# Second roundings behind the masks, banks by age, thresholds of the first steps on ScalarE, and a piece of MLP work between turning and values

## The chip, the cores and the metric

The kernel runs on one core of a Trainium2 chip. The metric is the device time in microseconds of one execution. The profile comes from one execution of its own; its span runs from the first to the last instruction.

## What is computed

Attention with a threshold, followed by a two-layer MLP with squared relu. There are 8 batches with 8 heads of 576 tokens and 64 channels, everything in float32:

```python
scores = scale * np.matmul(q, k.transpose(0, 1, 3, 2))          # scale = 1/8
thresh = np.max(scores, axis=-1, keepdims=True) - tau
scores = np.where(scores >= thresh, scores, -1000000000.0)
attn = np.exp(scores - np.max(scores, axis=-1, keepdims=True))
attn = attn / (np.sum(attn, axis=-1, keepdims=True) + 1e-09)
attn_out = np.matmul(attn, v)                                   # (8, 8, 576, 64)
x = attn_out.transpose(0, 2, 1, 3).reshape(4608, 512)
h = x @ w_in                                                    # (4608, 2048)
g = np.maximum(h, 0.0) ** 2
out = g @ w_out                                                 # (4608, 512)
```

## The kernel before

The order of the work on all engines is written out by hand. The attention is cut into **steps**. A step handles one block of 128 queries (the last block of a sequence has 64) of a pair of heads `u` = 0, 1, against all 576 keys. A **visit** is the run of steps over one pair of heads. The first four visits (steps 0 to 7) handle the first two blocks of each pair of batch 0, the next four (steps 8 to 19) its other three blocks; from step 20 on a visit covers all five blocks of a pair. There are 148 steps.

In each step TensorE makes the scores (L273, L280; later L296) in PSUM, VectorE takes the row maxima (`maxima`, L317), ScalarE makes the bias -maximum/8 and the exponents (`early_exponents`, L332 and L333, or `exponents`, L339 to L342), and VectorE masks: `threshold` keeps an exponent where the score reaches the threshold "maximum - 8 tau" and sums the row (L354), then takes the larger of the sum and a small constant (L356) and its reciprocal (L357). GpSimd divides (`divide`: a small L362, then L364 for each head). Two steps later TensorE turns the quotients (`turn`, L408, L415, L421), in three parts whose PSUM results ScalarE copies to `wT` (L409, L417, L422), and three steps after a block or group of blocks the values are multiplied in (`mix`, L524) and copied to `xT` (L507). From step 35 on turning goes through DRAM instead.

The threshold comes from two places. Steps 0 to 10 call `early_exponents`, where VectorE adds `ntau8`, which holds -8 tau in two columns, to the two maxima (L329); all later steps call `exponents`, where ScalarE does it with `AF.Identity` and `ntau8` as bias (L340).

The MLP's weights are read and rounded in 32 **weight pieces**: 16 of `w_in`, 16 of `w_out`. `round_weights(p, stage)` has five stages: 0 is two ScalarE operations (L149, L150), 1 a shift on VectorE (L152), 2 a mask of bits on VectorE (L154), 3 a product on GpSimd (L156), 4 an addition on GpSimd (L158). Then `load_weights` fetches piece p + 3 through SP's queue. In steps 3, 5, 7, 8 and 9 stage 0 of one piece is made; its other stages follow in the next step (4, 6, 8, 9, 10), behind `threshold` and `divide` in program order. From step 11 on a step does all stages of its own pieces: one piece, or two in steps 12, 15, 18 and 22. There stage 1 of all pieces stands ahead of `threshold`, except where the next visit's operands are turned in that step (`lay`), and stages 2 and 3 stand behind it.

The MLP itself works on chunks of 256 tokens, in **pieces of MLP work** of about the same TensorE time, queued in `waiting`. Chunk 0 has 16 pieces `mlp_in` (L571, with relu L581 and square L582 behind every second one) and 16 pieces `mlp_out` (L753, stored by L759 at the last two). A piece carries the number of weight pieces that must have been rounded; `state["usable"]` holds the count of one step ago. A planner works out how much MLP work a step gets (`rate`, with PIECE_US = 1.76 as the price of a piece), in quarters: `fill(quarter)` makes pieces as long as `state["left"]` is at least half a piece. In a middle step (11 to 39) the order is: scores, turning of parts 0 and 1, exponents, the first `fill`, `mix` if one is due, turning of part 2, masks, then the other three `fill`s and the division.

PSUM has eight banks. The turning takes banks 4 and 5 in the middle steps. Chunk 0's MLP work takes 6 and 7 in turn, through `take("mm", (6, 7))`. Later chunks call `next_bank`, which takes the longest unused bank of those allowed from the list `oldest`; `take` doesn't enter its banks in that list.

Of the kernel before, what the change touches and what calls it, by code (L numbers as in the profile page):

```python
# [9 lines left out]
FP32 = mybir.dt.float32  # L10
U32 = mybir.dt.uint32
AF = mybir.ActivationFunctionType
ALU = mybir.AluOpType
# [6 lines left out]
def kernel(  # L20
# [10 lines left out]
    nc = tc.nc  # L31
# [3 lines left out]
    P = 128  # L35
# [11 lines left out]
    SCALE = 0.125  # L47
# [7 lines left out]

    ident = const.tile([P, P], FP32, name="ident")
    seen = const.tile([P, 1], FP32, name="seen")
    ntau8 = const.tile([P, 2], FP32, name="ntau8")

    w_in_sb = const.tile([P, NMC, d_ff], FP32, name="w_in_sb")  # L60

# [19 lines left out]
    at = RAW * 2 * WP  # L81
# [56 lines left out]
    def round_weights(i, stage):  # L138

        words = weight_area(i).bitcast(U32).rearrange("p (n w) -> p n w", w=2)
        lo, hi = words[:, :, 0], words[:, :, 1]
        t, e, d = (turned[:, (i % 3 * 3 + x) * WP:(i % 3 * 3 + x + 1) * WP] for x in range(3))
        tu, eu = t.bitcast(U32), e.bitcast(U32)
        if stage == 0:
            nc.scalar.activation(out=e, in_=hi.bitcast(FP32), func=AF.Prelu, scale=2.0 ** -112, alpha=-2.0 ** 32)  # L149
            nc.scalar.activation(out=d, in_=lo, func=AF.Copy, scale=2.0 ** -52)  # L150
        elif stage == 1:
            nc.vector.tensor_scalar(out=tu, in0=eu, scalar1=3, scalar2=None, op0=ALU.logical_shift_left)  # L152
        elif stage == 2:
            nc.vector.tensor_scalar(out=eu, in0=tu, scalar1=0xFF800000, scalar2=None, op0=ALU.bitwise_and)  # L154
        elif stage == 3:
            nc.gpsimd.tensor_tensor(out=d, in0=d, in1=e, op=ALU.mult)  # L156
        else:
            nc.gpsimd.tensor_tensor(out=weight_piece(i)[1], in0=t.rearrange("p (h d) -> p h d", h=2),  # L158
                                    in1=d.rearrange("p (h d) -> p h d", h=2), op=ALU.add)
# [166 lines left out]
    def early_exponents(vis, i):  # L326

        w, sc, st = weights[vis, i]
        nc.vector.tensor_tensor(out=st[:, 1, 0:len(sc)], in0=st[:, 0, 0:len(sc)], in1=ntau8[:, 0:len(sc)], op=ALU.add)  # L329
        for u in range(len(sc)):  # L330
            bias = st[:, 2, u:u + 1]
            nc.scalar.activation(out=bias, in_=st[:, 0, u:u + 1], func=AF.Copy, scale=-SCALE)  # L332
            nc.scalar.activation(out=w[:, u, :].rearrange("p (h k) -> p h k", h=2), in_=sc[u],  # L333
                                 func=AF.Exp, bias=bias, scale=SCALE)

    def exponents(vis, i):
        w, sc, st = weights[vis, i]
        mx, thr, bias = (st[:, j, 0:len(sc)] for j in range(3))
        nc.scalar.activation(out=bias, in_=mx, func=AF.Copy, scale=-SCALE)  # L339
        nc.scalar.activation(out=thr, in_=mx, func=AF.Identity, bias=ntau8[:, 0:1])  # L340
        for u in range(len(sc)):
            nc.scalar.activation(out=w[:, u, :].rearrange("p (h k) -> p h k", h=2), in_=sc[u],  # L342
                                 func=AF.Exp, bias=bias[:, u:u + 1], scale=SCALE)

    def threshold(vis, i):

        w, sc, st = weights[vis, i]
        n = len(sc)  # L350
        thr, sm, den, rcp = (st[:, j, 0:n] for j in (1, 3, 5, 6))
        for u in range(n):
            wu = w[:, u, :].rearrange("p (h k) -> p h k", h=2)
            nc.vector.scalar_tensor_tensor(out=wu, in0=sc[u], scalar=thr[:, u:u + 1], in1=wu,  # L354
                                           op0=ALU.is_ge, op1=ALU.mult, accum_out=sm[:, u:u + 1])
        nc.vector.tensor_reduce(out=den, in_=st[:, 3:5, 0:n].rearrange("p j u -> p u j"), axis=AX.X, op=ALU.max)  # L356
        nc.vector.reciprocal(rcp, den)  # L357

# [11 lines left out]

    def take(what, among):
        used[what] += 1
        return bank[among[used[what] % len(among)]]

    def next_bank():

# [5 lines left out]
    def last_used(x):  # L382
        oldest.remove(x)
        oldest.append(x)
# [472 lines left out]
    mixes = {}  # L857
# [51 lines left out]
    def rate(s):  # L909


        if s < out_from:
            return (PIECE_US * sum(x[2] == 0 for x in waiting) + sum(early_values(x) for x in range(s, out_from))) / (out_from - s) - early_values(s)
        have = PIECE_US * len(waiting) - state["left"]
        best = 1e9
        at = s
        for e in sorted(chunk_at) + [END]:
            if e > s:
                have += sum(other(x) for x in range(at, e))
                at = e  # L920
# [36 lines left out]
    def fill(us):  # L957
        state["left"] += us
        while waiting and state["left"] >= PIECE_US / 2 and waiting[0][0] <= state["usable"]:
            piece()  # L960
        state["left"] = min(state["left"], PIECE_US)
# [57 lines left out]

    load_qk(0)  # L1020
    make_identity(nc, ident)
    nc.gpsimd.dma_start(out=ntau8[:, 0:1], in_=tau.to_broadcast([P, 1]))
    nc.gpsimd.memset(qmid, 0.0)
    for t in vs:
        for u in range(2):
# [6 lines left out]
    load_v(0)  # L1032
    for i in range(RAW):
        load_weights(i)
    for x in (1, 0):
        nc.gpsimd.tensor_scalar(out=ntau8[:, x:x + 1], in0=ntau8[:, 0:1], scalar1=-1.0 / SCALE, scalar2=None, op0=ALU.mult)
    keep_busy(20, 7)
    done = 0
    rounded_by = [0]
# [89 lines left out]
    def early_step(s):  # L1129


        n, i = steps[s]
        first, last = i == visits[n][1][0], i == visits[n][1][-1]
        now = list(range(sum(pieces[:s]), sum(pieces[:s + 1])))
        if first and n and n + 2 < 2 * HP:
            load_qk(n + 2)
        if s == 0:
            scores(0)()
            early_exponents(n, i)
            keep_busy(18, 7)  # L1140
# [12 lines left out]
        if s == 2:  # L1153
            keep_busy(12, 4)
        if s > 1 and (first or n >= HP and i == FIRST + 1) and not (first and n >= HP):
            prep_part(k, n + 1)
        if s > 1 and last:
            prep_part(q, n + 1)
        for fn in copies:
            fn()  # L1160
        if s in mixes:
            mix(*mixes[s])
            for j in chunk_at.get(s, ()):
                add_chunk(j)
        if first:
            split_left(n)
        for p in now:
            round_weights(p, 0)
        threshold(n, i)
        divide(n, i)  # L1170
        while rounding:
            p = rounding.popleft()
            for stage in (1, 2, 3):
                round_weights(p, stage)
            end_rounding(p)
        rounding.extend(now)
        assert s < early_to - 1 or not now
        if first and n:
            load_v(n)

    rounding = deque()
    for s in range(END + 1):
# [37 lines left out]
        if on:  # L1220
            exponents(n, i)
            if s and by_dma(steps[s - 1][0]):
                turn_last(s)
            for p in now[1:]:
                round_weights(p, 0)
            if at == 1:
                split_left(n)
            if lay:
                prep(n + 1)
            elif now:  # L1230
                for p in now:
                    round_weights(p, 1)
        if s in mixes and not old:
            mix(*mixes[s])
            for j in chunk_at.get(s, ()):
                add_chunk(j)
        quarter = rate(s) / 4 if s < END else 1e9
        fill(quarter)
        if s in mixes and old:
            mix(*mixes[s])  # L1240
            for j in chunk_at.get(s, ()):
                add_chunk(j)
# [8 lines left out]
        if on:  # L1251
            threshold(n, i)
            for fn in prep_at[s] + load_at[s]:
                fn()
            if lay and now:
                round_weights(now[0], 1)
            if now:
                round_weights(now[0], 2)
                round_weights(now[0], 3)
            for p in now[1:]:  # L1260
                assert not lay
                round_weights(p, 2)
                round_weights(p, 3)
            if not at_once:
                divide(n, i)
# [60 lines left out]
```

## Time and profile before

| what | us |
|---|---|
| median of 3 runs (lowest to highest) | 1328.32 (1327.66 to 1328.34) |
| the profiled execution | 1329.19 |
| its span | 1327.4 |
| TensorE (PE) busy | 1292.5 |
| VectorE (DVE) busy | 936.9 |
| GpSimd (POOL) busy | 786.3 |
| ScalarE (ACT) busy | 582.4 |

"Busy" is the time in which the engine has at least one instruction under way. L354 is line 354 of the kernel before. A name such as `w<-big,st,w` gives what is written and what is read: `big` is the PSUM tile, `st` the small statistics of a step, `turned` the work area of the rounding, `wo` the second weight matrix and, early on, spare room. PEld is the loading of weights into TensorE. The wait ahead of an instruction is given with the work that ended it. The exponents of one head take 741 ns on ScalarE in the early steps, the mask 805 ns on VectorE, the division 919 ns on GpSimd on the mean.

### The profile page before, as it was taken

To read this page: it belongs to the slowest core of one execution; us is meant where nothing else is said; L and a number is where in the kernel's file an instruction comes from. 1 tells how busy PE (TensorE), PEld (TensorE's weight loads), DVE (VectorE), ACT (ScalarE), POOL (GpSimd) and SP (SyncE) were. 2 spreads that over 40 slices of the span, in tenths; PEclk is the share of its full clock that TensorE was granted. 3 is DMA by queue.
4 is the path that set the end of the run, shared out by engine and by line. 5 is a ranking of instruction groups with operands and counts; after the bars stand their busy time and mean duration, and the time that the engine had idled before them with its cause. 6 is when DMAs were issued, how large, how long until landed. Compare 5 with 4: busy or idle time off the path is not lost.

```text
span 1327.4 us, 24734 instructions
## 1 busy us (share of the span) xinstructions
PE 1292.5 (97%) x8862; PEld 1070.4 (81%) x8862; DVE 936.9 (71%) x2037; ACT 582.4 (44%) x1342; POOL 786.3 (59%) x917
## 2 busy tenths in 40 slices
PE   7899999999999999999999999999999999999998
PEld 5666556888887879697878888888887988889997
DVE  6978876887787878778776777868686877622131
ACT  4777774335352626253534353434343434331321
POOL 3789974874846564565665655646574737454351
PEclk9999999999999999999999999999999999999999
DMA  6764531757687869676766867767686766520000
GB/s 128 154 160 121 152 85 26 166 134 178 166 188 168 196 152 207 146 195 157 151 165 159 181 152 180 174 126 180 146 194 135 189 161 153 160 53 9 9 17 17
DMA packets 320907, 185.48 MB, mean 140 GB/s; under 512 B 282224, under 2 KB 282256, under 8 KB 314384
## 3 DMA queue, kind: packets, MB, share of 16 engines
q1 hardware_dynamic: 309120, 115.78, 46.1%
q0 software_dynamic: 10000, 67.92, 12.8%
q8 instruction: 70, 1.15, 0.4%
q14 instruction: 53, 0.43, 0.1%
q10 hardware_dynamic: 1664, 0.21, 0.1%
HBM read 108.04 MB, written 68.42 MB: 133 GB/s over the span
## 4 chain that ended last, share of the span: by engine, by line
PE 83%; DVE 6%; DMA 4%; ACT 2%; POOL 2%; issue 2%; SPq 1%; DVEq 0%; ACTq 0%; POOLq 0%
PE big L682 29%; PE big L788 28%; PE big L524 10%; PE big L296 8%; PE big L571 3%; PE big L280 2%; DVE st L317 2%; DMA wT<-aside 1%; PE big L753 1%; DMA aside<-turned 1%; DVE w L354 1%; PE big L408 1%; SPq L185 1%; ACT w L342 1%; POOL w_in_sb L158 0%
## 5 line engine op out<-in xcount | busy, mean ns | idle before, releaser
L354 DVE SCALAR_TENSOR_TENSOR w<-big,st,w 128x576 f32<-128x576 f32 x269 | 207.1, 805 | 88.1 <-ACT w L342 87.6
L317 DVE TENSOR_REDUCE st<-big 128x1 f32<-128x576 f32 x288 | 204.3, 748 | 88.8 <-PE big L296 60.7
L364 POOL TENSOR_SCALAR w<-w,st 128x576 f32<-128x576 f32 x269 | 244.9, 919 | 27.8 <-DVE st L357 22.3
L788 PE MATMUL big<-wo,gsum 128*128 128x256 f32 x1088 | 243.8, 382 | 0.0
L788 PEld LDWEIGHTS big<-wo,gsum 128*128 128x128 f32 x1088 | 204.4, 190 | 37.0 <-issue 7.6
L682 PE MATMUL big<-xT,w_in_sb 128*128 128x128 f32 x1536 | 187.4, 277 | 1.3 <-DVE g L694 1.2
L682 PEld LDWEIGHTS big<-xT,w_in_sb 128*128 128x128 f32 x1536 | 178.5, 192 | 10.5 <-issue 7.7
L788 PE MATMUL big<-wo,g 128*128 128x256 f32 x816 | 185.3, 382 | 0.1
L342 ACT ACTIVATE w<-big,st 128x576 f32<-128x576 f32 x255 | 174.2, 734 | 0.2 <-POOL t L659 0.2
L788 PEld LDWEIGHTS big<-wo,g 128*128 128x128 f32 x816 | 151.6, 190 | 26.1 <-issue 6.5
L524 PE MATMUL big<-wT,vs 128*64 128x256 f32 (+5 forms) x1420 | 159.6, 389 | 5.8 <-DMA wT<-aside 3.7
L524 PEld LDWEIGHTS big<-wT,vs 128*64 128x64 f32 (+1 forms) x1420 | 85.6, 136 | 71.7 <-issue 20.7
L362 POOL TENSOR_SCALAR st<-st 128x2 f32<-128x2 f32 (+1 forms) x148 | 35.6, 241 | 181.2 <-DVE w L354 169.8
L339 ACT ACTIVATE st<-st 128x2 f32<-128x2 f32 (+1 forms) x137 | 27.9, 204 | 250.1 <-DVE st L317 248.8
L430 POOL DMA_DIRECT2D aside<-turned x50 | 29.9, 597 | 177.9 <-DVE turned L459 171.8
L694 DVE TENSOR_TENSOR g<-big,g 128x512 f32<-128x512 f32 x96 | 64.7, 677 | 83.4 <-PE big L682 77.8
L296 PE MATMUL big<-kT,qT 64*128 64x256 f32 (+3 forms) x768 | 106.9, 416 | 0.0
L296 PEld LDWEIGHTS big<-kT,qT 64*128 64x128 f32 x768 | 84.5, 186 | 14.5 <-issue 5.0
L690 ACT ACTIVATE g<-g 128x512 f32<-128x512 f32 x96 | 60.3, 628 | 63.7 <-DVE g L694 63.6
L561 POOL TENSOR_TENSOR gsum<-g 128x512 f32<-128x512 f32 x34 | 46.1, 1356 | 69.8 <-ACT g L691 60.2
L691 ACT ACTIVATE g<-g 128x512 f32<-128x512 f32 x128 | 80.7, 630 | 4.1
L453 DVE STREAM_TRANSPOSE turned<-w 128x512 f32<-128x512 f32 x100 | 70.3, 703 | 0.3 <-issue 0.3
(118 smaller groups left out, 2063.4 us busy)
## 6 DMA issues: line engine op xcount, KB each, us to landing
aside<-turned POOLq DMA_DIRECT2D x50, 1152.0 KB, 4.8
wT<-aside SPq DMA_DIRECT2D x200, 288.0 KB, 5.4
vs<-in_v_dram SPq DMA_DIRECT2D x72, 128.0 KB, 5.9
wo<-in_moe_w_in_dram SPq DMA_DIRECT2D x16, 512.0 KB, 4.4
wo<-in_moe_w_out_dram SPq DMA_DIRECT2D x16, 512.0 KB, 3.6
out_dram<-osb POOLq DMA_DIRECT2D x32, 256.0 KB, 4.1
kl<-in_k_dram SPq DMA_DIRECT2D x113, 72.0 KB, 3.4
ql<-in_q_dram SPq DMA_DIRECT2D x112, 72.0 KB, 5.8
```

Source lines behind the costliest of these rows:

```text
L296: nc.tensor.matmul(big[to, at + x0:at + x1], lhsT, keys[u * D:(u + 1) * D, x0:x1], start=True, stop=True)
L317: nc.vector.tensor_reduce(out=mx[:, u:u + 1], in_=sc[u], axis=AX.XY, op=ALU.max)
L342: nc.scalar.activation(out=w[:, u, :].rearrange("p (h k) -> p h k", h=2), in_=sc[u], func=AF.Exp, bias=bias[:, u:u + 1], scale=SCALE)
L354: nc.vector.scalar_tensor_tensor(out=wu, in0=sc[u], scalar=thr[:, u:u + 1], in1=wu, op0=ALU.is_ge, op1=ALU.mult, accum_out=sm[:, u:u + 1])
L364: nc.gpsimd.tensor_scalar(out=w[:, u, :], in0=w[:, u, :], scalar1=z[:, u:u + 1], scalar2=rcp[:, u:u + 1], op0=ALU.add, op1=ALU.mult)
L453: move(wb[:, 0:h, :, :], whole_[:, 0, :, :, :])
L524: nc.tensor.matmul(ps[u * D:(u + 1) * D, :], vs[n % 2][rows, u * (NBLK + 1) + c, :], wT[rows, at // REST:(at + ps.shape[1]) // REST, NBLK ...
L682: nc.tensor.matmul(to[:, f, :], factor(j, p, q, c)[:, f * P:(f + 1) * P], part[:, c, :], start=(p in "125" and f == 0 and c == 0), stop=(p ...
L690: nc.scalar.activation(out=to, in_=to if src is None else src, func=AF.Relu)
L691: nc.scalar.activation(out=to, in_=to, func=AF.Square)
L694: nc.vector.tensor_tensor(out=x, in0=to, in1=x, op=ALU.add)
L788: nc.tensor.matmul(to, left[:, f, :], wo[:, slot, f, :], start=(f == 0), stop=(f == HF - 1))
```

## The change

There are four edits in it.

First, the early steps make their threshold on ScalarE: L329 goes, and one `AF.Identity` operation for both heads is put behind the exponent of head 0. `ntau8` shrinks to one column, so one of GpSimd's two small operations that fill it goes.

Second, roundings change their place behind the masks. In steps 0 to 10 stages 1 and 2 of the previous step's piece are called inside `threshold`, between the masks and the maximum of the sums; stages 3 and 4 stay where they are. From step 11 on stage 1 of a step's second piece moves from ahead of the masks to a place behind them, next to its stage 2.

Third, `take("mm", ...)` enters its bank in the list `oldest`, so that `next_bank` knows of it.

Fourth, in a middle step with both a turning and values due, a piece of MLP work is made ahead of `mix` if the first `fill` made none and the next piece's weights are usable.

```diff
     def early_exponents(vis, i):
 
         w, sc, st = weights[vis, i]
-        nc.vector.tensor_tensor(out=st[:, 1, 0:len(sc)], in0=st[:, 0, 0:len(sc)], in1=ntau8[:, 0:len(sc)], op=ALU.add)
         for u in range(len(sc)):
             bias = st[:, 2, u:u + 1]
             nc.scalar.activation(out=bias, in_=st[:, 0, u:u + 1], func=AF.Copy, scale=-SCALE)
             nc.scalar.activation(out=w[:, u, :].rearrange("p (h k) -> p h k", h=2), in_=sc[u],
                                  func=AF.Exp, bias=bias, scale=SCALE)
+            if u == 0:
+                nc.scalar.activation(out=st[:, 1, 0:len(sc)], in_=st[:, 0, 0:len(sc)], func=AF.Identity, bias=ntau8)
...
-    def threshold(vis, i):
+    def threshold(vis, i, between=()):
...
             nc.vector.scalar_tensor_tensor(out=wu, in0=sc[u], scalar=thr[:, u:u + 1], in1=wu,
                                            op0=ALU.is_ge, op1=ALU.mult, accum_out=sm[:, u:u + 1])
+        for fn in between:
+            fn()
         nc.vector.tensor_reduce(out=den, in_=st[:, 3:5, 0:n].rearrange("p j u -> p u j"), axis=AX.X, op=ALU.max)
         nc.vector.reciprocal(rcp, den)
...
     def take(what, among):
         used[what] += 1
-        return bank[among[used[what] % len(among)]]
+        at = among[used[what] % len(among)]
+        if what == "mm":
+            last_used(at)
+        return bank[at]
...
-    for x in (1, 0):
-        nc.gpsimd.tensor_scalar(out=ntau8[:, x:x + 1], in0=ntau8[:, 0:1], scalar1=-1.0 / SCALE, scalar2=None, op0=ALU.mult)
+    nc.gpsimd.tensor_scalar(out=ntau8, in0=ntau8, scalar1=-1.0 / SCALE, scalar2=None, op0=ALU.mult)
...
-        threshold(n, i)
+        threshold(n, i, [lambda p=p, x=x: round_weights(p, x) for p in rounding for x in (1, 2)])
         divide(n, i)
         while rounding:
             p = rounding.popleft()
-            for stage in (1, 2, 3):
-                round_weights(p, stage)
+            round_weights(p, 3)
             end_rounding(p)
...
             elif now:
-                for p in now:
-                    round_weights(p, 1)
+                round_weights(now[0], 1)
...
         quarter = rate(s) / 4 if s < END else 1e9
+        made = state["made"]
         fill(quarter)
+        if s in mixes and old and state["made"] == made and waiting and waiting[0][0] <= state["usable"]:
+            piece()
         if s in mixes and old:
             mix(*mixes[s])
...
             for p in now[1:]:
                 assert not lay
+                round_weights(p, 1)
                 round_weights(p, 2)
                 round_weights(p, 3)
```

More of the change, by code (lines that the diff above doesn't have):

```diff
@@ L57 @@
     seen = const.tile([P, 1], FP32, name="seen")
-    ntau8 = const.tile([P, 2], FP32, name="ntau8")
+    ntau8 = const.tile([P, 1], FP32, name="ntau8")
     w_in_sb = const.tile([P, NMC, d_ff], FP32, name="w_in_sb")
@@ L339, in exponents @@
         nc.scalar.activation(out=bias, in_=mx, func=AF.Copy, scale=-SCALE)
-        nc.scalar.activation(out=thr, in_=mx, func=AF.Identity, bias=ntau8[:, 0:1])
+        nc.scalar.activation(out=thr, in_=mx, func=AF.Identity, bias=ntau8)
         for u in range(len(sc)):
@@ L1021 @@
     make_identity(nc, ident)
-    nc.gpsimd.dma_start(out=ntau8[:, 0:1], in_=tau.to_broadcast([P, 1]))
+    nc.gpsimd.dma_start(out=ntau8, in_=tau.to_broadcast([P, 1]))
     nc.gpsimd.memset(qmid, 0.0)
```

## The prediction

> **What bounds the kernel now.** I read the page first: busy time, then the slices, then the chain.
>
> ```profile
> PE 1292.5 (97%) x8862; PEld 1070.4 (81%) x8862; DVE 936.9 (71%) x2037; ACT 582.4 (44%) x1342; POOL 786.3 (59%) x917
> ...
> PE   7899999999999999999999999999999999999998
> ...
> PE 83%; DVE 6%; DMA 4%; ACT 2%; POOL 2%; issue 2%; SPq 1%; DVEq 0%; ACTq 0%; POOLq 0%
> ```
>
> TensorE bounds the whole, so time is won only where TensorE has holes, and the first slices (33 us each) have them. The windows cut at the stages of the schedule show who paces each:
>
> ```profile
> 0.00:66.00 66.00, 51.56 (x392) 40.33 (x393) 52.41 (x122) 39.85 (x95) 36.19 (x62) 0.95 0.68 141
> 66.00:156.00 90.00, 84.53 (x492) 56.94 (x491) 74.77 (x151) 68.32 (x159) 80.86 (x84) 1.00 0.54 145
> 156.00:212.00 56.00, 53.14 (x328) 30.75 (x326) 41.37 (x96) 38.50 (x94) 40.59 (x47) 1.00 0.35 80
> 212.00:400.00 188.00, 187.88 (x1265) 156.01 (x1263) 142.66 (x314) 74.13 (x177) 117.16 (x134) 1.00 0.66 152
> ```
>
> After the two times come PE, PEld, DVE, ACT and POOL busy. Steps 0 to 10 (to 66 us) are VectorE's (9.5 of each 10 us from 30 to 60); steps 11 to 25 are GpSimd's (80.9 of 90, 9.3 to 9.8 of each 10 us from 80 to 130); from 156 on TensorE leads, and from 212 it has practically no hole. Whatever the front gains therefore moves the rest forward: the pieces of MLP work are counted out by the planner, not by time.
>
> Next I read the rows that the diff touches, line by line (shortest, median and longest duration in ns, then first and last start):
>
> ```profile
> L329 DVE TENSOR_TENSOR st<-st,ntau x11: 160/161/1236, 10.9 to 60.0; 128x2 f32<-128x2 f32 x10, 128x1 f32<-128x1 f32 x1
> ...
> L154 DVE TENSOR_SCALAR turned<-turned x32: 406/634/1529, 32.9 to 200.8; 128x512 uint32<-128x512 uint32 x32
> ```
>
> and their neighbours in the timeline (start, duration, in brackets the wait ahead and its releaser):
>
> ```profile
> 42.77 1.79 POOL L364 TENSOR_SCALAR w<-w,st 128x576 f32<-128x576 f32 x2 [0.28 <-PE big L280]
> 42.93 0.94 DVE L154 TENSOR_SCALAR turned<-turned 128x512 uint32<-128x512 uint32 x1
> ...
> 44.53 1.27 POOL L156 TENSOR_TENSOR turned<-turned 128x512 f32<-128x512 f32 x1
> ...
> 45.23 0.59 DVE L329 TENSOR_TENSOR st<-st,ntau 128x2 f32<-128x2 f32 x1
> ...
> 74.97 0.43 DVE L152 TENSOR_SCALAR turned<-turned 128x512 uint32<-128x512 uint32 x1 [2.01 <-ACT turned L149]
> 75.32 0.81 DVE L354 SCALAR_TENSOR_TENSOR w<-big,st,w 128x576 f32<-128x576 f32 x1
> ...
> 77.67 2.62 POOL L156 TENSOR_TENSOR turned<-turned 128x512 f32<-128x512 f32 x2 [2.59 <-DVE turned L154]
> ...
> 96.31 2.62 POOL L156 TENSOR_TENSOR turned<-turned 128x512 f32<-128x512 f32 x2 [0.36 <-DVE turned L154]
> ...
> 210.94 0.59 ACT L759 COPY osb<-big 128x512 f32<-128x512 f32 x1
> ...
> 211.59 5.45 PE L571 MATMUL big<-xT,w_in_sb 128*128 128x256 f32 x24 [1.06 <-ACT osb L759]
> ```
>
> The same tiny addition (L329) takes 160 ns or 1236 ns. At 45.23 it ends at 45.82, as GpSimd's L156 does (44.53 + 1.27 = 45.80). L154 stretches from 0.41 to 0.94 under GpSimd's divisions L364.
>
> **What the Trainium skill says.** "SBUF — State Buffer", section "SBUF: two separate sides": VectorE and GpSimd share a port pair under an exclusive lock, taken by a VectorE op in a two-port mode or with two SBUF inputs, and held for the whole instruction. The rows above agree. "VectorE: DVE Perf Modes", section "Why PSUM operands drop a tier": an operand in PSUM keeps an op out of the two-port mode. The trace agrees: masks (L354, 805 ns) and maxima (L317, 748 ns) stay within some per cent beside a busy GpSimd.
>
> **Part 1, thresholds of steps 0 to 10 on ScalarE.** Removed: eleven L329, 4.1 us in all (seven of 0.16, 0.58 to 0.59 in steps 5, 7 and 9, 1.24 in step 10), and one of GpSimd's two L1036 (0.28, hidden). Added: eleven ScalarE operations of 0.28 (the row of L340), no new table (one load in the trace, and L340 uses the same function). In a step with a key transpose (L254, 0.78 us) behind the maxima VectorE binds and gains some 0.25. Where only the short query transpose stands there, the mask waits for the threshold: exponent start + 0.64 (the spacing to the next small operation) + 0.28, against 0.74 for the exponent alone, so it starts 0.2 later; the second exponent starts 0.11 later (L339 to L340: 65.91, 66.01). Queued behind the new operation are the second bias and exponent, then the copies of L409. Steps 3 and 8: about -0.1 each. Steps 5 and 7, whose L329 was locked out, win 0.3, as the exponents then bind.
>
> **Part 2, stages 1 and 2 ahead of the sums' maximum in the early steps.** Nothing is added; L152 and L154 (0.41 + 0.43) move ahead of L356 and L357, so the divisions start 0.84 later, behind them L156 and L158 on GpSimd. That is covered: `turn` reads the quotient two steps later. Four of the five L154 took 0.94, locked out by the divisions; now these haven't started: 0.44 won each. But in steps 9 and 10, where rounding follows rounding, the later L158 and L156 still run when stages 1 and 2 come up (some 0.8 and 1.5 us of lock-out), so these two steps give back nearly all they win.
>
> Sum of parts 1 and 2 up to step 10: +0.2 (steps 0 to 2), -0.1, +0.64 (step 4), +0.3, +0.7 (step 6), +0.3, -0.15, +0.3 for steps 8 to 10: 2.2; step 11 begins nearer its own chain (scores L280 0.9 earlier against step 8, of which 0.35 pass): **2.5 us**. From below 0 (loads pace the front, rival B), from above 4 (no lock-out in steps 9 and 10).
>
> **Part 3, second rounding behind the masks, steps 12, 15, 18, 22.** In step 12 the mask (75.32) stood behind the second L152 (74.97), which waited 2.01 for ScalarE's L149, though its exponent was there at 73.7. So masks and first L154 come 1.6 earlier. The second L154 then falls into the first L156 and waits out its 1.27; the second L156 ends near 79.1 for 80.3: **1.2 us** of GpSimd's hole of 2.59 go. In steps 15 and 18 the hole was 0.36, and the second L154 now has to slip in behind a running L156: **0.3 us lost** in each, bounds 0.2 won and 0.5 lost. Behind it on VectorE stand the next step's maxima, 1.3 later; I cost that at nothing, because ScalarE there waits for GpSimd (1.33 before L150 at 102.62); without this cover it costs up to 1.3 each. Step 22: TensorE (PE L280 at 138.05) is already the limit; nothing.
>
> **Part 4, a piece ahead of the values.** By the planner's arithmetic (PIECE_US, `rate`, `usable`) the condition holds in steps 22, 24, 26, 27 and 29 alone: in 13, 16 and 19 the next piece's weights aren't rounded. Steps 22, 24, 26 and 27 fill TensorE's wait for L409 or L417 (weight-load idle 0.48, 0.48, 0.54, 0.48); step 29 had a piece there. Steps 25 and 30 lose the piece that covered their third turning: 0.4 each. The pieces' ScalarE and GpSimd work is nil here (`mlp_out` before its last two). Net 1.98 - 0.8 = 1.2, of which I take **0.9**; bounds 0 and 2.
>
> **Part 5, banks by age.** At 211.59 the first piece of chunk 1 writes bank 6, which L759 empties last (210.94 + 0.59). By age it takes bank 7, free at 209.60. TensorE is next held by the turning before it (to 210.53): **1.0 us**, bounds 0.5 and 1.1. Afterwards banks 6 and 7 only swap roles.
>
> SP's DMA issues keep their order; GpSimd's stage 3 and its queue behind it keep theirs.
>
> **Sum**: 2.5 + 1.2 - 0.6 + 0.9 + 1.0 = 5.0 us. The profiled execution took 1329.19 (span 1327.4), so 1324.2; the median of the runs is 0.87 below it: **1323.3 us**, 0.38% less. A measurement of this kernel can tell some 0.2% (2.7 us) from no change.
>
> **Rivals.** A: GpSimd's holes ahead of L156 all close. Between 66 and 156 us it waited 6.6 us for L154; if stage 2 always slips between two GpSimd operations, parts 1 to 3 give 7 and the total is 9: 1319.3. Against it: GpSimd's operations stand back to back there. Chance 0.12.
>
> B: loads pace the front. The chain of waits up to 66 us names SP's issues (L185, 15.2%) and landings. Then parts 1 and 2 give nothing, and 2.5 remain: 1325.8, no measurable change. Against it: VectorE's own idle before L254 is 0.3 us in all for keys; only the first query transpose waited 6.2. With other small outcomes 0.15.
>
> C, slower: lock-outs follow the moved stages. Each stage that comes up in the middle of a GpSimd operation waits up to 1.27 for it, and behind it stand now the sums' maximum, reciprocal and division (early) or the next maxima (middle). Five early and four middle roundings with two lock-outs of 1.1 each are 20 us of VectorE time against the 4.1 + 4 x 0.5 = 6.1 that it loses; if half reaches the path, the front costs some 4 net of what it wins, and with parts 4 and 5 paid in: 1331.5. It decides from the point where more than about eight lock-outs reach the path; I count four that might. Chance 0.13.
>
> That the change doesn't do what it says is excluded for part 5 and possible for part 4, where the planner could have had nothing usable; five places are what it has.
>
> **Numbers.** Forecast (faster, 1320 to 1325.6) 0.60, A 0.12, no change 0.15, C 0.13. Faster 0.72, same 0.15, slower 0.13. The range 1318.5 to 1329.0 takes in A, the forecast's own range and B, and leaves out most of C.
>
> **What would show it.** Right: no L329; L154 near 0.43 in steps 4, 6 and 8; scores of step 11 (PE L280, 62.45 before) near 60; GpSimd's double L156 of step 12 from 77.7 to about 73.5; L571 of chunk 1 without the wait for L759; L524 in steps 22, 24, 26, 27 without its wait. Wrong: L152 and L154 of steps 4 to 10 longer than before; PE L280 of step 11 within 1 us of 62.45; the first L571 of chunk 1 no earlier than 210.

## The result, and the profile after

The changed kernel takes 1323.25 us (median; 1322.47 to 1324.31) where the kernel before, run beside it, takes 1328.30: a ratio of 0.9963, with a 95% interval of 0.9951 to 0.9975. The profiled execution took 1324.21 us with a span of 1322.4 us, against 1329.19 and 1327.4 before: 5.0 us less, the sum that was forecast. How the sum came about is another matter.

In the changed kernel the lines are shifted: the threshold on ScalarE is L335 (early) and L341 (later), the mask L355, the maximum of the sums L359, the reciprocal L360, the division L367, turning L414, its copy L415, the values L530, `mlp_in` L577, `mlp_out` L759 and its store's copy L765. L152, L154, L156, L158, L273, L280 and L317 keep their numbers.

The busy times on the page of the changed kernel:

```profile
PE 1294.1 (98%) x8862; PEld 1070.3 (81%) x8862; DVE 938.8 (71%) x2026; ACT 584.3 (44%) x1353; POOL 786.0 (59%) x916
```

VectorE has eleven operations fewer and ScalarE eleven more, and yet VectorE is not less busy: what it saved it spends waiting inside instructions that are locked out. L152 and L154 of the sixteen weight pieces of steps 11 to 22 take 34.1 us together, for 25.2 before. The windows say where (after the two times: PE, PEld, DVE, ACT, POOL busy, then TensorE's clock):

```profile
0.00:66.00 66.00, 55.45 (x406) 43.19 (x407) 51.06 (x117) 44.28 (x112) 36.28 (x61) 0.95 0.69 142
66.00:156.00 90.00, 85.61 (x501) 56.07 (x501) 81.81 (x152) 68.16 (x160) 83.68 (x87) 1.00 0.57 149
156.00:212.00 56.00, 55.06 (x330) 33.30 (x328) 37.93 (x91) 36.70 (x87) 40.99 (x47) 1.00 0.33 83
```

By 66 us TensorE has done 3.9 us more (51.56 before). From 66 to 156 us GpSimd is 2.8 us and VectorE 7 us busier. From 156 to 212 us TensorE shows 1.9 us more busy time, and some of that is no work, as will be seen.

The timeline of the changed kernel (start, duration, in brackets the wait ahead) shows the moved roundings in steps 6, 9, 10 and 12, in this order:

```profile
40.83 0.43 DVE L154 TENSOR_SCALAR turned<-turned 128x512 uint32<-128x512 uint32 x1
...
54.52 0.90 DVE L152 TENSOR_SCALAR turned<-turned 128x512 uint32<-128x512 uint32 x1
...
58.89 0.59 DVE L152 TENSOR_SCALAR turned<-turned 128x512 uint32<-128x512 uint32 x1
59.52 1.39 DVE L154 TENSOR_SCALAR turned<-turned 128x512 uint32<-128x512 uint32 x1
...
72.70 1.40 POOL L156 TENSOR_TENSOR turned<-turned 128x512 f32<-128x512 f32 x1 [0.36 <-DVE turned L154]
73.00 1.39 DVE L154 TENSOR_SCALAR turned<-turned 128x512 uint32<-128x512 uint32 x1
74.53 1.28 POOL L156 TENSOR_TENSOR turned<-turned 128x512 f32<-128x512 f32 x1 [0.43 <-ACT g L587]
```

In step 6 stage 2 takes 0.43 us for 0.94 before. In steps 9 and 10 the stages are locked out. In step 12 the second stage 2 (73.00) waits out GpSimd's first product, and the pair of products, one block of 2.62 us before, falls into two with a hole of 0.43 us; it ends at 75.81 us for 80.29.

The ruler for the rest is the start of each step's scores in both traces. Before minus after, in us:

| scores of step | 3 | 4 | 6 | 8 | 9 | 11 | 12 | 22 | 24 | 26 | 27 | 28 | 31 | 35 | 36 |
|---|---|---|---|---|---|---|---|---|---|---|---|---|---|---|---|
| earlier by | 0.87 | 0.72 | 1.65 | 2.61 | 2.41 | 3.42 | 3.40 | 4.19 | 4.77 | 4.37 | 4.16 | 4.47 | 4.16 | 4.16 | 5.48 |

5.5 us stay until late in the kernel; 5.0 are left at the end.

**A disturbance to be kept apart.** The windows of the kernel before show TensorE's clock (the last number but two) fall around step 11:

```profile
60.00:62.00 2.00, 0.42 (x8) 0.18 (x4) 1.97 (x3) 1.89 (x5) 1.92 (x3) 1.00 0.91 255
62.00:64.00 2.00, 1.55 (x9) 0.74 (x9) 1.47 (x6) 1.49 (x4) 1.81 (x3) 0.81 0.89 139
64.00:66.00 2.00, 2.00 (x11) 1.67 (x10) 1.76 (x3) 0.95 (x3) 1.92 (x3) 0.50 0.51 80
66.00:68.00 2.00, 2.00 (x10) 1.75 (x9) 1.04 (x3) 2.00 (x7) 0.93 (x1) 0.84 0.89 225
```

Half the clock for (0.19 + 0.50 + 0.16) x 2 / 0.5 = 3.4 us, behind a stretch in which TensorE was hardly busy (0.42 of 2 us). The Trainium skill, "TensorE: Matmul & The Clock Gate", section "Part 1: The HAM clock gate (the "warmup" mystery)", says that the clock is halved after an idle window of some 3.4 us, that it is full again after a busy one, and that the windows run freely. The measured 3.4 us agree with the length of one window. But the stretch ahead was not idle, and how busy it is does not decide alone: in the 3.4 us ahead of the dip TensorE was busy for 1.38 us before and for 1.66 us in the changed kernel, while two kernels below with 1.71 and 1.67 us at this place (the one with another order of the second roundings, and the same without the piece) have no dip there. (All these stretches are counted in steps of 3.4 us from the half clock that every trace shows near 20 us.) The profiled execution of the changed kernel has the same dip at 59 to 63 us, so the table compares like with like. Some of the executions below have none at this place. Against a trace with the dip that shows as 1.26 us at step 12 (0.7 to 0.8 of it left later), and I take it off. The beginning scatters too: among the kernels below that keep L329, the scores of step 3 lie between 0.45 us behind and 1.67 us ahead of the kernel before.

### The profile page after: what moved, and what is told of

The parts are those of the page before. It is cut to its first block, busy times and chain, and to the rows that moved or that the text cites. A ratio compares the mean times of both kernels' runs of the same rounds, so it can differ in the third digit from the quotient of the medians.

```text
span 1322.4 us, 24730 instructions
## 1 busy us (share of the span) xinstructions
PE 1294.1 (98%) x8862; PEld 1070.3 (81%) x8862; DVE 938.8 (71%) x2026; ACT 584.3 (44%) x1353; POOL 786.0 (59%) x916
## 4 chain that ended last, share of the span: by engine, by line
PE 84%; DVE 4%; DMA 3%; ACT 2%; POOL 1%; issue 1%; SPq 0%; DVEq 0%; POOLq 0%; ACTq 0%
PE big L688 29%; PE big L794 28%; PE big L530 10%; PE big L296 8%; PE big L577 4%; PE big L280 2%; PE big L759 2%; DMA wT<-aside 1%; DMA aside<-turned 1%; PE big L414 1%; DVE st L317 1%; DVE w L355 1%; ACT w L343 1%; POOL w_in_sb L158 0%; PE big L273 0%
## 5 line engine op out<-in xcount | busy, mean ns | idle before, releaser
L355 DVE SCALAR_TENSOR_TENSOR w<-big,st,w 128x576 f32<-128x576 f32 x269 | 207.8, 807 | 88.9 <-ACT w L343 86.6
L317 DVE TENSOR_REDUCE st<-big 128x1 f32<-128x576 f32 x288 | 204.3, 748 | 84.6 <-PE big L296 61.1
L367 POOL TENSOR_SCALAR w<-w,st 128x576 f32<-128x576 f32 x269 | 243.7, 914 | 29.4 <-DVE st L360 24.5
L530 PE MATMUL big<-wT,vs 128*64 128x320 f32 (+5 forms) x1420 | 159.8, 389 | 5.4 <-DMA wT<-aside 3.5
L530 PEld LDWEIGHTS big<-wT,vs 128*64 128x64 f32 (+1 forms) x1420 | 85.5, 136 | 73.7 <-issue 20.5
```

Of the source, the lines that this page charges most:

```text
L317: nc.vector.tensor_reduce(out=mx[:, u:u + 1], in_=sc[u], axis=AX.XY, op=ALU.max)
L367: nc.gpsimd.tensor_scalar(out=w[:, u, :], in0=w[:, u, :], scalar1=z[:, u:u + 1], scalar2=rcp[:, u:u + 1], op0=ALU.add, op1=ALU.mult)
L530: nc.tensor.matmul(ps[u * D:(u + 1) * D, :], vs[n % 2][rows, u * (NBLK + 1) + c, :], wT[rows, at // REST:(at + ps.shape[1]) // REST, NBLK ...
```

## The experiments

The theory was the sum of the prediction: VectorE's saved time carries the front, GpSimd's hole in step 12 the middle, TensorE's waits for the turned quotients the stretch behind, one bank wait chunk 1. The rivals were that the loads pace the front, that lock-outs eat the gain, and, from the table above (nothing won from step 22 to step 31), that the piece ahead of the values only moves a wait.

### Thresholds alone

The kernel before with the first edit only:

```diff
-        nc.vector.tensor_tensor(out=st[:, 1, 0:len(sc)], in0=st[:, 0, 0:len(sc)], in1=ntau8[:, 0:len(sc)], op=ALU.add)
+            if u == 0:
+                nc.scalar.activation(out=st[:, 1, 0:len(sc)], in_=st[:, 0, 0:len(sc)], func=AF.Identity, bias=ntau8[:, 0:1])
```

> The kernel before with the first edit alone: the thresholds of steps 0 to 10 on ScalarE. Theory 'locks': the addition on VectorE cost 0.16 us a step and, in four steps, up to 1.1 us of waiting for GpSimd; both go, and the exponents bind in the short steps. Scores of step 11 begin 2.3 to 3 us earlier than 62.45, and the run takes 2 to 3 us less than before. Rival 'length only': only the eleven times 0.16 us count, since what waits behind a lock waits for something else anyway: 1 us or less at step 11. Rival 'loads': the front is paced by its loads: step 11 stays within 0.3 us.

1326.35 us against 1328.67, ratio 0.9984 (0.9977 to 0.9991). In the trace the scores of step 11 start 1.53 us earlier, and 2.3 us from step 13 on, of which 0.75 are the missing dip: **1.6 us**. That is less than the 2.3 to 3 us of the theory and more than the 1 us of "length only". Half of it, 0.79 us, is there by the scores of step 3, and ahead of them no L329 had been locked out. VectorE's transpose of the keys in step 0, in the kernel before and in this one:

```profile
11.23 0.78 DVE L254 STREAM_TRANSPOSE kT<-wo 128x576 f32<-128x576 f32 x1
...
10.61 0.77 DVE L254 STREAM_TRANSPOSE kT<-wo 128x576 f32<-128x576 f32 x1
```

The maxima ahead of it end at 10.82 and at 10.69 us. The addition took 0.16 us, but maxima and transpose were 0.41 us apart with it, and without it the transpose follows at once. Nor is this a lucky start. Take the traces whose step 0 begins within 0.04 us of the kernel before: at step 3 the five with this edit are 0.79 to 1.11 us ahead of it, the four without lie between -0.45 and 0.03.

### Early stages alone

The kernel before with stages 1 and 2 between masks and sums in steps 4, 6, 8, 9 and 10 only:

```diff
+        for fn in between:
+            fn()
         nc.vector.tensor_reduce(out=den, in_=st[:, 3:5, 0:n].rearrange("p j u -> p u j"), axis=AX.X, op=ALU.max)
...
-        threshold(n, i)
+        threshold(n, i, [lambda p=p, x=x: round_weights(p, x) for p in rounding for x in (1, 2)])
...
-            for stage in (1, 2, 3):
-                round_weights(p, stage)
+            round_weights(p, 3)
```

> The kernel before with one half of the second edit alone: stages 1 and 2 of the early roundings between masks and the maximum of the sums, the threshold's addition still on VectorE. Theory 'locks': L154 falls from 0.94 to 0.43 in steps 4, 6 and 8, and steps 9 and 10 give back what they win: scores of step 11 begin 0.5 to 1.2 us earlier than 62.45, and the run gains about as much. Rival 'slower by locks': the moved stages meet the addition and the multiplication of the rounding before, in more than three steps, and step 11 is not earlier or later than before.

1324.84 us, ratio 0.9973 (0.9964 to 0.9983). Step 11 starts 2.13 us earlier: **2.1 us**, more than the 0.5 to 1.2 expected, and 2.37 us counted from step 3, whose scores come 0.23 us later here. L329 is still there, and its row shows where some of the surplus comes from (shortest, median and longest, ns):

```profile
L329 DVE TENSOR_TENSOR st<-st,ntau x11: 160/336/695, 11.1 to 58.4; 128x2 f32<-128x2 f32 x10, 128x1 f32<-128x1 f32 x1
```

The longest was 1236 ns, in step 10, where L329 came up at 60.03 us, just after GpSimd had begun a product (L156 at 59.99). With the roundings moved, the divisions start later, L329 meets their end and takes 0.34 us. (In steps 6 and 8 it is the other way round: 0.69 and 0.64 us for 0.16.) The two edits thus compete for one lock-out. From step 3 to step 11, without the scatter of the beginning, they gain 0.74 and 2.37 us alone, 3.1 in sum, and 2.56 together in the changed kernel. The missing half microsecond lies in step 10: 0.13 and 0.72 us alone, 0.28 together.

### One tensor less for the threshold

The kernel before with L329 reading one tensor and a column as a scalar:

```diff
-        nc.vector.tensor_tensor(out=st[:, 1, 0:len(sc)], in0=st[:, 0, 0:len(sc)], in1=ntau8[:, 0:len(sc)], op=ALU.add)
+        nc.vector.tensor_scalar(out=st[:, 1, 0:len(sc)], in0=st[:, 0, 0:len(sc)], scalar1=ntau8[:, 0:1], scalar2=None, op0=ALU.add)
```

> The kernel before with the threshold's addition still on VectorE, but with the constant as a per-partition scalar in place of a second tensor, so that it has one tensor input. If it is the second input from SBUF that is locked out by GpSimd, it takes 0.16 to 0.2 us in all eleven steps, the four long ones among them, and the scores of step 11 begin 1 to 2 us earlier than 62.45. If an operation with one tensor input on so few elements is locked out as well (as L154 is, on 512 columns), the long ones stay at 0.6 and 1.2 us and step 11 doesn't move. Nothing of the result changes.

1327.99 us in one execution. Only step 10 is shorter, by 0.47 us (from 0.45 behind the kernel before at its scores to 0.02 ahead at step 11's). For two columns the lock stays: 0.59 to 0.60 us in steps 5, 7 and 9. In step 10, with one column, it does not, though GpSimd's product has just begun:

```profile
60.49 0.21 DVE L329 TENSOR_SCALAR st<-st,ntau 128x1 f32<-128x1 f32 x1
...
60.45 1.26 POOL L156 TENSOR_TENSOR turned<-turned 128x512 f32<-128x512 f32 x1
```

The Trainium skill ("SBUF — State Buffer", section "SBUF: two separate sides") names two ways into the lock, a two-port mode and two SBUF inputs. The runs agree with the second way: 1.24 us for the one-column addition of two tensors, 0.21 for the same addition with one. The two-column addition of one tensor, locked out all the same, would have to be of the first way; no trace shows in which mode an operation ran. Of the 1.0 us won in that instruction 0.47 pass on; then the mask waits for the exponent (0.37 us, at 61.55).

### Second roundings alone

The kernel before with stage 1 of the second piece behind the masks (steps 12, 15, 18, 22):

```diff
-                for p in now:
-                    round_weights(p, 1)
+                round_weights(now[0], 1)
...
             for p in now[1:]:
+                round_weights(p, 1)
                 round_weights(p, 2)
                 round_weights(p, 3)
```

> The kernel before with the other half of the second edit alone: stage 1 of a step's second piece behind the masks, in steps 12, 15, 18 and 22. The prediction: 1.2 us of GpSimd's wait ahead of the double L156 of step 12 go, 0.3 are lost in each of steps 15 and 18, so scores of step 21 begin 0.3 to 0.9 us earlier relative to those of step 12. Rival 'only the wait moves': what step 12 wins is lost again in steps 15, 18 and 22 by the second L154 waiting out the first L156, 0 or slower.

1327.59 us, ratio 0.9992 (0.9983 to 1.0000). Both traces have the dip. The gain is 0.03 us at step 12, 0.44 at step 13, 0.96 at step 21 and 0.93 from step 31 on: **0.9 us**. Two lines of its timeline, step 12:

```profile
76.04 1.40 POOL L156 TENSOR_TENSOR turned<-turned 128x512 f32<-128x512 f32 x1 [0.98 <-DVE turned L154]
77.87 1.27 POOL L156 TENSOR_TENSOR turned<-turned 128x512 f32<-128x512 f32 x1 [0.43 <-ACT g L581]
```

The hole is cut from 2.59 to 0.98 + 0.43 us, and the second product ends at 79.14 us, as the prediction had worked out. Steps 15 and 18 lose nothing: there the pair of products gets one hole of 0.43 us in place of one of 0.36 (in the changed kernel at 93.27).

### The piece ahead of the values alone

```diff
+        made = state["made"]
         fill(quarter)
+        if s in mixes and old and state["made"] == made and waiting and waiting[0][0] <= state["usable"]:
+            piece()
         if s in mixes and old:
```

> The kernel before with the fourth edit alone, a piece of MLP work ahead of the values in steps 22, 24, 26, 27 and 29. The prediction: 0.9 us earlier from step 31 on. Rival, from the trace of the changed kernel: 0.2 to 0.3 are won in steps 22, 24 and 27, but steps 25 and 27, which have less work between the scores and the next scores, let TensorE wait for the masks, and steps 31 and later begin within 0.2 us of what they would without the edit. Between steps 22 and 31 the two kernels are compared, so that the front doesn't matter.

1328.82 us, ratio 1.0001 (0.9992 to 1.0010). Against the kernel before its trace stands at -0.42 at step 22, -0.11 at 23, -0.40 at 24, -1.81 at 25 (where a piece of 1.7 us stands ahead of the point that is read), -0.72 at 26 and -0.93 from step 29 on: a **loss of 0.5 us**, neither the prediction's gain nor the even result of the rival. What TensorE does in steps 26 and 28, in this kernel and then in the one before (step 26):

```profile
155.70 1.73 PE L280 MATMUL big<-kT,qT 64*128 64x288 f32 x7
...
167.24 1.73 PE L280 MATMUL big<-kT,qT 64*128 64x288 f32 x8
```

```profile
152.84 0.49 PE L408 MATMUL big<-ident,w 128*128 128x128 f32 x3
153.17 1.88 PE L753 MATMUL big<-wo,g 128*128 128x512 f32 x4
154.98 1.24 PE L280 MATMUL big<-kT,qT 64*128 64x288 f32 x8
...
156.92 2.38 PE L524 MATMUL big<-wT,vs 128*64 128x256 f32 x20 [0.40 <-ACT wT L417]
```

The scores' products take 1.73 us for 1.24 (in step 28 for 1.42). The weight loads of the changed kernel in the same place (step 26) say why:

```profile
150.61 0.29 PEld L280 LDWEIGHTS big<-kT,qT 64*128 64x128 f32 x2 [0.94 <-DVE wo L355]
151.35 0.54 PEld L280 LDWEIGHTS big<-kT,qT 64*128 64x128 f32 x5 [0.45 <-DVE wo L355]
```

The scores of head 1 wait in the middle of the row, until VectorE's mask has emptied the bank. Such a wait counts as busy in the windows: 0.3 of the 1.9 us that TensorE's busy time gained from 156 to 212 us is the row of step 28 (1.73 us in the changed kernel too, 1.42 before). Before, the step ahead had a piece (L753 at 153.17) between its turning and these scores, and in that time the mask was made. The same goes for step 25's third turning, which in the changed kernel waits 0.24 us for the copy of the second (148.24, for L415) where the piece of 151.12 stood in between before. This edit alone also loses 0.29 us in step 23, which the changed kernel does not; why stays open.

### The changed kernel without the piece

```diff
-        made = state["made"]
         fill(quarter)
-        if s in mixes and old and state["made"] == made and waiting and waiting[0][0] <= state["usable"]:
-            piece()
```

> The changed kernel without its fourth edit (no piece ahead of the values). Rival 'the piece gives nothing': time within 0.3 us of the changed kernel's, 5 us below the kernel before; the span between the scores of steps 22 and 31 (53.0 us in the changed kernel, 52.6 in the one before) is 52.4 to 52.9. The prediction's value for the edit would make it 0.9 us slower than the changed kernel.

1322.20 us, ratio 0.9953 (0.9936 to 0.9969). From step 22 to step 31 its lead goes from 5.67 to 5.72 us, where with the piece it goes from 4.19 to 4.16, and in a second execution of the changed kernel from 5.92 to 5.91. In the changed kernel, then, the piece costs under 0.1 us: by the step starts with and without it, it wins 0.31 us in each of steps 22 and 27, and loses 0.18 in steps 24 and 25 together, 0.22 in step 26 and 0.31 in step 28. It takes away the waits ahead of the values and gives them back in the scores and turnings behind. The 1 us between the two medians is not the piece's: the profiles of this kernel and of the second execution have spans of 1320.3 and 1320.4 us.

### Banks by age alone

```diff
-        return bank[among[used[what] % len(among)]]
+        at = among[used[what] % len(among)]
+        if what == "mm":
+            last_used(at)
+        return bank[at]
```

> The kernel before with the third edit alone, banks by age. The theory: only the first piece of chunk 1 is touched; it no longer waits 1.06 us for the copy of the last rows of chunk 0, nothing up to 210 us moves, the rest is 1.0 to 1.3 us earlier. Rival: the wait only moves to the second bank or to the next scores, and the run gains under 0.3 us.

1327.19 us, ratio 0.9990 (0.9982 to 0.9999). Between the scores of steps 35 and 36 the lead jumps from 1.08 to 2.40, **1.3 us**, and from step 13 on nothing else moves. Ahead of that the two traces differ by no edit: this one is 1.67 us ahead at step 3, has its dip at 47 to 51 us, which takes 1.62 us of the lead, and none at step 11. In the changed kernel (TensorE and ScalarE, from the timeline) `mlp_in` of chunk 1 no longer waits for the copy that it waited 1.06 us for:

```profile
205.88 0.49 PE L414 MATMUL big<-ident,w 128*128 128x128 f32 x3
206.21 2.97 PE L577 MATMUL big<-xT,w_in_sb 128*128 128x256 f32 x13
```

```profile
206.78 0.59 ACT L765 COPY osb<-big 128x512 f32<-128x512 f32 x1
```

### Another order of the second roundings

The changed kernel with stage 1 of the second piece, then both stages 2, then both stages 3, so that GpSimd's two products stay together:

```diff
-                round_weights(now[0], 2)
-                round_weights(now[0], 3)
             for p in now[1:]:
                 round_weights(p, 1)
-                round_weights(p, 2)
-                round_weights(p, 3)
+            for p in now:
+                round_weights(p, 2)
+            for p in now:
+                round_weights(p, 3)
```

> The changed kernel with another order of the moved roundings in steps 12, 15, 18 and 22: stage 1 of the second piece first, then both stages 2, then both stages 3, so that no stage 2 comes up while GpSimd multiplies the first piece. If the lock on the shared port is what the second L154 waits for, its 1.37 us in steps 12, 15 and 18 become some 0.4 to 0.9, GpSimd's two L156 stand back to back there, and the run is 0.3 to 1 us faster than the changed kernel. If GpSimd's total work alone sets the pace there, the maxima come earlier but the time stays within 0.3 us.

1322.87 us, ratio 0.9954 (0.9939 to 0.9969), which the interval can't tell from the changed kernel. The products are one block again (2.62 us at 72.28), the second stage 2 no longer waits alone for 1.37 us, and from step 12 to step 22 the lead grows by 0.38 us (4.96 to 5.34), where the dip-free execution of the changed kernel gains 0.03 (5.89 to 5.92). That one started 1 us ahead, and how much of a lead this stretch can take up is not known. The other traces without the dip say the same and have the same flaw: the two kernels with this order below gain 0.47 and 0.71 us in these steps from leads of 4.4 and 4.9, the kernel without the piece loses 0.04 from a lead of 5.7. So the 0.4 us stay a hint.

### Towards a better version

Three kernels on one chip: the changed kernel without the piece and with the other order; the same with the early stages between masks and sums in steps 4, 6 and 8 only; and the changed kernel.

> The changed kernel without the piece of MLP work ahead of the values (as in the kernel without that piece, 1322.2 us) and with the second roundings in the order of the kernel with another order (stage 1 of the second half of w_in, then both stages 2, then both stages 3). If the two gains add, with the piece's 0.5 to 1.0 us and the order's 0.4 us, it takes 1321.8 to 1322.4 us, 0.5 to 1.4 us less than the changed kernel on the same chip. If the order matters only because the piece was there to be delayed, it is the kernel without the piece again, 1322.2 to 1322.9 us.

> The kernel of the run before in this call, with steps 9 and 10 of the front given back their early stages' place behind the division: the stages stand between masks and sums only in steps 4, 6 and 8, where they took 0.43 us each. If the lock-outs of the moved stages in steps 9 and 10 (0.90, 0.59 and 1.39 us instead of 0.43) lie on the path, it is 0.3 to 0.8 us faster than the run before. If what stands behind the division then locks out the next division or the last rounding, as in the kernel before, it is 0 to 0.7 us slower.

```diff
-        threshold(n, i, [lambda p=p, x=x: round_weights(p, x) for p in rounding for x in (1, 2)])
+        threshold(n, i, [lambda p=p, x=x: round_weights(p, x) for p in rounding for x in (1, 2) if s < 9])
...
             p = rounding.popleft()
+            if s >= 9:
+                round_weights(p, 1)
+                round_weights(p, 2)
             round_weights(p, 3)
```

> The changed kernel itself, beside the two others of this call on the same chip: 1322.9 to 1323.6 us, a ratio of 0.9963 to the kernel before.

Against 1327.98 us for the kernel before: 1322.22 (ratio 0.9954, 0.9941 to 0.9968), **1321.22** (0.9947, 0.9935 to 0.9960) and 1322.85 us (0.9959, 0.9946 to 0.9971). The first is no answer: the number lies where both expectations overlap. The second beats the kernel before and the changed kernel: its slowest execution (1321.48) is below the fastest of the changed kernel (1321.88). The first two differ in steps 9 and 10 alone. VectorE and GpSimd there, with the stages between masks and sums:

```profile
54.80 0.88 DVE L152 TENSOR_SCALAR turned<-turned 128x512 uint32<-128x512 uint32 x1
...
59.16 0.59 DVE L152 TENSOR_SCALAR turned<-turned 128x512 uint32<-128x512 uint32 x1
59.79 1.39 DVE L154 TENSOR_SCALAR turned<-turned 128x512 uint32<-128x512 uint32 x1
...
61.63 0.82 POOL L367 TENSOR_SCALAR wo<-wo,st 128x576 f32<-128x576 f32 x1 [0.37 <-DVE st L360]
```

and with the old place in these two steps:

```profile
54.91 0.52 DVE L152 TENSOR_SCALAR turned<-turned 128x512 uint32<-128x512 uint32 x1
55.47 0.43 DVE L154 TENSOR_SCALAR turned<-turned 128x512 uint32<-128x512 uint32 x1
...
59.03 1.23 DVE L152 TENSOR_SCALAR turned<-turned 128x512 uint32<-128x512 uint32 x1
60.29 0.43 DVE L154 TENSOR_SCALAR turned<-turned 128x512 uint32<-128x512 uint32 x1
...
60.45 0.96 POOL L367 TENSOR_SCALAR wo<-wo,st 128x576 f32<-128x576 f32 x1
```

The stages take 2.61 us for 3.29, and nothing of it stands ahead of the sums: the division of step 10 starts 1.2 us earlier, of which 0.2 are the start of this execution. Step 11 begins 0.3 us earlier by the steps (0.5 with the start), step 36 0.55 us (0.76 with the start). The two traces end 1.6 us apart, but what is added behind step 36 can't be traced to these steps. Nor can the 1.0 us between the medians be put down to them: the executions of the first lie between 1321.06 and 1323.42 us, those of the second between 1321.06 and 1321.48.

## Why the prediction was right

The direction, the size and most places were right; the terms were not, and their errors cancel. The sum against the dip-to-dip trace:

| part | forecast | changed kernel | alone |
|---|---|---|---|
| 1 and 2, to step 11 | 2.5 | 3.4 | 1.53 + 2.13 |
| 3, steps 12 to 22 | 0.6 | 0.8 | 0.9 |
| 4, steps 22 to 35 | 0.9 | 0.0 | -0.5 |
| 5, step 35 to 36 | 1.0 | 1.3 | 1.3 |
| sum | 5.0 | 5.5, at the end 5.0 | 5.4 |

**Parts 1 and 2.** Most steps came as counted: steps 4 and 5 gave 0.93 us (forecast 0.94), 6 and 7 gave 0.96 (1.0), step 8 -0.20 (-0.15). Two terms were forecast too small. The larger is "+0.2 (steps 0 to 2)": they gave 0.9. The addition, in the way of the key transpose of step 0, was worth 0.41 us of VectorE's time there and not its own 0.16 or the 0.25 counted. The other is "these two steps give back nearly all they win": steps 9 and 10 gave 1.01 us where the sum has 0.3, or 0.65 with the 0.35 that it allows step 11's start. The lock-outs did come, at 0.90, 0.59 and 1.39 us, but by the run with the old place in these steps they cost 0.3 of step 11, since the mask of step 10 waits 0.93 us for ScalarE anyhow. The scores of step 11 came at 59.03 for "near 60".

**Part 3.** Step 12 came as described; its first product starts at 72.70 for "about 73.5" because the front came earlier, and it is no longer a double. The mis-sized term is the loss of 0.3 in each of steps 15 and 18: the new hole of 0.43 us is bigger than the old one of 0.36 by 0.07 only, and the old one is gone. Why 0.44 at step 13 of that edit alone become 0.96 by step 21 was not settled.

**Part 4** is the step that failed. The waits ahead of the values went: from 126 to 185 us TensorE's own waits name none for L530, where before they named 0.7 us for L409 and 0.4 for L417. So they were worth 1.1 us; the 1.98 of the prediction was idle time of the weight loads, which run ahead of the products. What it did not ask is what else the moved piece had covered. It charged 0.4 each in steps 25 and 30 for the turning, and nothing for the masks: it asked what the pieces mean for ScalarE and GpSimd ("nil here"), and not what VectorE had finished under them, and the longer scores of steps 26 and 28 with step 25's turning took the gain back.

**Part 5** won 1.3 us for 1.0 (bound 1.1): the turning was taken to hold TensorE to its last end, but the first products of the piece start 0.33 us behind the turning's start (206.21 against 205.88), inside its 0.49 us.

**The rivals.** That GpSimd's holes all close didn't come: it still waits 4.3 us for L154 between 66 and 156 us for 6.6, and most of the fall is step 12. That loads pace the front is refuted, since two edits to VectorE's work alone move step 11 by 1.5 and 2.1 us, the first of them step 3 by 0.8. The slower case had its mechanism right and more of it than was counted: beside the three early lock-outs and the second stage 2 of steps 12, 15, 18 and 22 (1.37 to 1.39 us each), the second stage 1 of steps 15, 18 and 22 takes 1.26 us for 0.80 to 0.87, and in steps 13, 16 and 19, where nothing was moved, L154 takes 1.37 us for 0.77 to 0.93. These are most of the 8.9 us by which L152 and L154 have grown in steps 11 to 22. What it had wrong is that half would reach the path; steps 12 to 22 still gained 0.8 us. (Its own sum, 4 us lost and 1.9 won, makes 1330.4 and not 1331.5.)

The medians of the single edits add to 8.6 us (2.3 + 3.8 + 1.1 - 0.1 + 1.5), the whole change to 5.0. In traces the parts add to 5.4 and 5.5. The clock's dip explains part of the difference at most. The traces of the first two edits lack it at step 11, which is worth 0.7 to 0.8 us each; but the mean clocks of the executions speak against it as a reason for the medians. Of the twenty executions with the first edit eleven have a mean clock of 0.998 of full speed, which only traces without the dip show, and eight have 0.996 or less; their medians are 1326.37 and 1326.29 us. With the third edit all twelve executions have 0.996 or less, as most traces with the dip. So the rest is not settled, nor whether a shorter hole ahead of step 11 makes the dip itself rarer.

## What to carry to other kernels

Work that fills an engine's wait covers other engines' work as well: before a piece is moved, list what each engine finishes during it, and read a row of matmuls that has become longer at the same clock as a wait. Where two engines lock each other out, an operation's cost is its place among the other's operations: move it to where the other hasn't started, and leave it where it would follow it into the next. Terms well under 1 us are read from step starts between traces with the same clock, counted from the last step ahead of the edit, not from medians that scatter by 1 us. And a short operation between two others can cost more than its length: look at the distance between its neighbours.

## What was not expected of the hardware

A VectorE operation that GpSimd locks out comes in at the end of the running operation, between two on GpSimd that otherwise have no hole: L154 of 73.00 ends 0.29 us after L156 of 72.70. (This L156 took 1.40 us for 1.27 itself, as it began while L152 ran, from 72.55 to 72.96.) The next L156 starts 0.43 us behind the first. That hole is no proof of the lock, since this L156 reads what L154 writes; the trace names L587 here and L154 at 93.27, and in all four steps with two pieces it starts 0.14 to 0.15 us behind L154's end. Where GpSimd's next operation needs nothing that VectorE has still to do, it starts at once and gets longer: behind L588, which locks out L152 from 80.78 to 81.93 us, L156 of 81.60 takes 1.46 us for 1.27.

An addition of one column with a single tensor input wasn't locked out at all (0.21 us), the same with two columns was (0.59); this is one execution. And the dip of TensorE's clock came at the same place in some executions of one kernel and not in others, for 1.26 us of step 11. In the trace with banks by age alone it came at 47 us, behind 3.4 us in which TensorE was busy for 2.26, and took 1.62 us.
